# Linear attention followed by a gated feed-forward: PSUM banks named in the order table, two banks per exponential, a finer start, and a last tile in columns

## Chip, cores and metric

One core of one Trainium2 chip. The metric is device microseconds of that core, from the first to the last instruction of one execution. A kernel is run several times and the median of all its runs is quoted. The runs of the kernel before lie within 0.3% of each other. Runs flagged slow (on one core: over 1.5% above the fastest of the same kernel) are left out of the ratios, but not of the medians. "Span" is the length of the one execution that was profiled; here it is some 2 us less than that same run's time.

Before: 393.23 us (392.9 to 394.07, 4 runs).

## The reference, cut to what matters

```python
q, k, v: (8, 8, 576, 64)      w_phi: (64, 128)      # batch, heads, sequence, head_dim
w_gate, w_val: (512, 1536)    w_out: (1536, 512)

def phi(x):
    proj = x @ w_phi
    proj = proj - max(abs(proj), axis=-1)            # kept per row
    return concatenate([exp(proj), exp(-proj)])      # 256 features
                                # (as written, the maximum is subtracted before the sign is turned)
kv  = einsum('bhsf,bhsd->bhfd', phi(k), v);  z = sum(phi(k), over s)
num = einsum('bhsf,bhfd->bhsd', phi(q), kv)
attn = num / (phi(q) . z + 1e-6)                     # (8, 8, 576, 64)

x   = attn.transpose(0, 2, 1, 3).reshape(4608, 512)
out = (relu(x @ w_gate) * (x @ w_val)) @ w_out       # (4608, 512)
```

With `m` the row's largest absolute value, the two halves of phi are `exp(p)·exp(-m)` and `exp(-p)·exp(m)`. So the kernels take the exponentials of the plain projection, and multiply the row factors `exp(-m)` and `exp(m)` into V, which is much smaller. These factors are the tile `ek`.

## The kernel before, in parts

Each batch has 576 positions: 512 are worked in four chunks of 128, and the other 64 (the "tail") of two batches make one mixed chunk. All instructions are issued in an order that was searched beforehand and is written down as a table; PSUM comes from one pool of eight banks.

```python
ORDER = """0 40 41 1 44 45 4 52 53 48 56 57 42 49 ... 735 736 737 738"""   # pieces, in order of issue
LOADS = """km0 q0 wv0 wg0 k1 wv1 wg1 v1 wv2 wg2 q1 wo qm0 k2 km1 vm1 v2 q2 ..."""
...
def order(self):                       # Plan: simulates engines; fills waits of PE with zero matmuls
    ...
        n = int((start - now - 0.25) / (0.43 if now < 8.0 else 0.22))
        if n > 0: ... yield lambda n=n: self.keep_busy(n)
...
def rows_group(T4):                    # K or Q times w_phi: one bank for each parity of heads
    banks = [psum_a(), psum_a()]
    for j in range(4):
        for par in range(2):
            rows = slice(D * par, D * (par + 1))
            nc.tensor.matmul(banks[par][:, F*j : F*(j+1)], lhsT=T4[rows, j, :], rhs=w2[rows, par, :])
    return banks

def k_group(st):
    banks = rows_group(st["T"])
    kp = st["kp"] = st["pool"].tile([P, 2, 4, 2, F], BF16, name="kp")
    for par in range(2):
        row_max(st["m"][:, par::2], banks[par])                     # DVE tensor_reduce, |.|, max
        for s, sign in ((0, 1.0), (1, -1.0)):
            nc.scalar.activation(kp[:, s, :, par, :], banks[par]..., AF.Exp, scale=sign)
    ek = st["ek"] = sb_s.tile([P, 8, 2], FP32, name="ek")
    for s, sign in ((0, -1.0), (1, 1.0)):
        nc.scalar.activation(ek[:, :, s], st["m"], AF.Exp, scale=sign)   # exp(-m), exp(m)

def scale_v(engs, dst, src, ek):       # on POOL: V times the row factors, for both signs
    ...  eng.tensor_tensor(dst[:, :, s, 0:D], src, ek[:, :, s:s+1]..., op=ALU.mult)
...
def q_finish(x, dst, by_dma): ...      # x for the feed-forward, turned by PE or by DMA
def out_step(t, part): ...             # the output projection; one copy on ACT, two stores on SP
...
load_kqv(0, "kn", k, nc.sync, ...)     # first loads; later loads are pieces of ORDER
...
```

From batch 2 on, K and Q are turned by a DMA transpose, issued by SP (`knT<-kn`), and not by PE.

Of the kernel before, what the change touches and what calls it, by code (L numbers as in the profile page):

```python
# [8 lines left out]
FP32 = mybir.dt.float32  # L9
BF16 = mybir.dt.bfloat16  # L10
# [6 lines left out]
FIRST = ((0, 2, 0, 6), (2, 4, 0, 6), (0, 4, 6, 12))  # L17


class Plan:  # L20







    LAG = dict(PE=0.33, ACT=0.2, DVE=0.14, POOL=0.15, SP=0.1, NONE=0.0, DMA=0.0)
    BUSY_TILL = 45.0

    def __init__(self, slots):
        self.slots = {tag: [0.0] * n for tag, n in slots.items()}
        self.free = dict.fromkeys(self.LAG, 0.0)
        self.done = {}
        self.mode = "PE"
        self.uses = {}
        self.pieces = []

    def add(self, rank, kind, fn, ops, needs=(), gives=None, take=(), drop=(), after=(), at=None):


        self.pieces.append((rank, len(self.pieces), fn, ops, needs, gives, take, drop, after, at))

    def times(self, piece):

        _, _, _, ops, needs, _, take, _, after, _ = piece
        if any(n not in self.done for n in needs) or any(n not in self.done for n in after):
            return None
        ready = max([0.0] + [self.done[n] for n in needs])
        for tag in set(take):  # L50
            held = self.slots[tag][: take.count(tag)]
            if len(held) < take.count(tag):
                return None
            ready = max([ready] + held)
        free = dict(self.free)
        ends, start = [], None
        for i, op in enumerate(ops):
            eng, us = op[:2]
            if eng in ("PE", "PE64"):
                us += 0.1 * (eng != self.mode)  # L60
                eng = "PE"
            src = op[2] if len(op) > 2 else i - 1
            t = max(free[eng], ready if src is None or not i else ends[src])
            if len(op) > 4:
                t = max(t, self.done[op[4]])
            if eng == "NONE":
                t = ready if src is None or not i else ends[src]
            if start is None:
                start = t
            free[eng] = t + us  # L70
            ends.append(t + us + (op[3] if len(op) > 3 else self.LAG[eng]))
        return start, ready, ends, free

    def emit(self, piece, got):
        _, _, fn, ops, _, gives, take, drop, _, at = piece
        _, _, ends, self.free = got
        if ops[0][0] in ("PE", "PE64"):
            self.mode = ops[0][0]
        for tag in take:
            self.slots[tag].pop(0)  # L80
        for tag, op, *shared in drop:
            if shared:
                n, key = shared
                ends_ = self.uses.setdefault((tag, key), [])
                ends_.append(ends[op])
                if len(ends_) < n:
                    continue
                self.slots[tag].append(max(ends_))
            else:
                self.slots[tag].append(ends[op])  # L90
        if gives is not None:
            self.done[gives] = ends[-1 if at is None else at]
        return fn

    def order(self):


        assert sorted(map(int, ORDER.split())) == list(range(len(self.pieces)))
        for i in map(int, ORDER.split()):
            piece = self.pieces[i]  # L100
            got = self.times(piece)
            assert got is not None
            now, start = self.free["PE"], got[0]
            if piece[3][0][0] in ("PE", "PE64") and start < self.BUSY_TILL and self.slots["pa"][0] <= now:
                n = int((start - now - 0.25) / (0.43 if now < 8.0 else 0.22))
                if n > 0:
                    self.slots["pa"].append(self.slots["pa"].pop(0))
                    got = self.times(piece)
                    yield lambda n=n: self.keep_busy(n)
            yield self.emit(piece, got)  # L110


ORDER = """0 40 41 1 44 45 4 52 53 48 56 57 42 49 6 46 7 54 58 50 60 14 2 61 71 3 55 43 82 86 62 59 51 5 47 10
83 87 63 64 65 67 90 84 68 69 72 73 9 94 66 88 85 70 13 8 133 74 75 403 404 76 405 78 79 406 407
408 409 410 11 411 80 412 95 89 413 77 109 81 91 98 414 415 416 417 131 418 419 99 420 421 92 422
96 423 93 100 424 425 426 427 97 428 429 127 12 134 128 101 17 142 102 103 430 105 120 431 432 121
433 434 435 106 146 436 437 438 107 110 439 111 440 104 441 442 108 112 135 15 443 116 113 114 444
16 117 445 18 446 132 172 118 447 138 448 122 115 129 449 450 19 119 130 143 144 139 123 451 452
453 454 21 455 456 457 147 150 458 140 182 459 124 136 460 461 161 145 151 148 462 125 463 174 20
141 23 152 464 137 149 212 175 465 153 154 183 22 176 466 467 155 178 186 179 468 469 157 470 471  # L120
184 472 473 162 185 180 158 159 474 173 177 156 163 160 187 475 223 476 164 165 188 213 477 168 478
225 169 214 479 166 238 170 167 171 189 181 480 215 481 190 216 219 25 191 482 483 192 234 484 235
24 485 217 486 193 194 487 220 26 488 489 195 490 226 491 239 27 126 227 221 240 492 493 236 230
197 494 495 496 497 201 498 499 196 202 500 501 218 231 224 222 502 264 278 198 503 504 237 505 228
203 506 232 507 508 199 509 510 200 233 208 29 209 242 229 210 511 270 204 512 274 513 205 241 243
266 206 514 211 207 515 516 244 271 517 518 28 519 265 245 520 246 521 267 282 279 31 522 249 30
253 523 293 315 304 247 524 32 525 526 527 250 272 528 529 254 530 531 280 532 255 268 275 533 534
281 251 535 260 536 537 248 33 318 538 539 540 276 541 256 261 262 542 252 257 543 544 269 326 317
263 545 546 277 258 283 259 327 547 548 549 550 284 551 552 273 553 311 319 34 35 312 554 285 555
37 316 556 286 557 558 36 287 289 559 560 288 290 322 561 294 562 563 356 305 328 564 330 565 295  # L130
323 313 320 566 567 366 568 296 569 570 297 571 572 39 300 573 574 298 575 321 576 345 577 291 578
301 579 580 324 581 302 582 306 331 292 329 299 303 583 358 584 585 307 334 586 362 332 587 588 335
367 589 38 590 333 308 396 591 592 325 397 336 593 594 309 595 337 596 597 310 357 341 363 359 338
598 599 364 600 360 601 602 603 339 370 604 605 606 607 314 371 608 609 610 372 368 611 346 612 342
613 343 347 614 615 340 616 617 618 348 344 352 353 361 354 369 619 620 621 349 350 385 622 374 623
355 351 375 624 625 373 626 627 376 628 629 365 630 381 382 383 631 377 632 633 634 635 386 636 637
638 387 639 640 641 642 392 643 378 393 379 644 645 646 647 648 649 650 651 652 380 653 654 394 388
384 389 390 655 395 656 657 391 658 398 659 660 661 399 400 662 663 664 665 666 667 668 669 670 671
672 673 674 675 676 677 678 679 680 681 682 683 684 685 686 687 688 689 690 401 691 402 692 693 694
695 696 697 698 699 700 701 702 703 704 705 706 707 708 709 710 711 712 713 714 715 716 717 718 719  # L140
720 721 722 723 724 725 726 727 728 729 730 731 732 733 734 735 736 737 738"""

LOADS = """km0 q0 wv0 wg0 k1 wv1 wg1 v1 wv2 wg2 q1 wo qm0 k2 km1 vm1 v2 q2 k3 v3 q3 qm1
k4 km2 vm2 v4 q4 k5 v5 q5 qm2 k6 km3 vm3 v6 q6 k7 v7 q7 qm3"""
# [3 lines left out]
def kernel(  # L148
# [24 lines left out]
    C = 4  # L173
# [15 lines left out]
    sb_k = ctx.enter_context(tc.tile_pool(name="sb_k", bufs=5))  # L189
    sb_kv = ctx.enter_context(tc.tile_pool(name="sb_kv", bufs=16))  # L190
    sb_s = ctx.enter_context(tc.tile_pool(name="sb_s", bufs=6))
    sb_x = ctx.enter_context(tc.tile_pool(name="sb_x", bufs=2))
    sb_h = ctx.enter_context(tc.tile_pool(name="sb_h", bufs=1))
    sb_g = ctx.enter_context(tc.tile_pool(name="sb_g", bufs=4))
    ps_a = ctx.enter_context(tc.tile_pool(name="ps_a", bufs=8, space=bass.MemoryType.PSUM))

    ctx.enter_context(tc.manual_schedule())

    def psum_a(dtype=FP32):
        n = 512 if dtype == FP32 else 1024  # L200
        return ps_a.tile([P, n], dtype, name="pa", tag="pa")
# [760 lines left out]
```

## Time and profile before

| reading | before |
|---|---|
| time, span | 393.23 us, 390.7 us |
| PE busy | 377.9 us, 97% |
| DVE, ACT, POOL busy | 251.6, 244.9, 156.1 us |
| first feed-forward matmul | 35.53 us |
| last matmul's start to the end | 5.20 us |

The page of the kernel before. Its first part gives each engine's busy time, share of the span and instruction count; in part 2 each digit is one fortieth of the span, in tenths of full clock; in part 5 a group of instructions has its count, its busy time and the mean of one in ns, then the engine's idle time ahead of the group.

```profile
span 390.7 us, 8804 instructions
...
PE 377.9 (97%) x3415; PEld 201.3 (52%) x3415; DVE 251.6 (64%) x570; ACT 244.9 (63%) x563; POOL 156.1 (40%) x202
...
PEclk9899999999999999999999999999999999999999
...
L321 ACT ACTIVATE kp<-pa 128x512 bf16<-128x512 f32 x144 | 74.6, 615 | 21.0 <-DVE mk L279 20.6
...
L279 DVE TENSOR_REDUCE mk<-pa 128x4 f32<-128x512 f32 x72 | 45.5, 682 | 7.0 <-PE pa L309 7.0
```

PE is the bound. ACT's 144 exponentials and DVE's 72 maxima of one bank each are long in sum, but ACT and DVE have idle time left. The small exponentials that make `ek`, two per group of K, are in the view of lines:

```profile
L329 ACT ACTIVATE ek<-mk 128x8 f32<-128x8 f32 x72 | 12.3, 244 | 0.0
```

The same execution by stretches: width of the stretch, busy time of PE, PEld, DVE, ACT and POOL with their instruction counts, clock, DMA share and GB/s.

```profile
0.00:26.00 26.00, 21.36 (x235) 12.19 (x236) 15.71 (x34) 17.62 (x45) 18.84 (x32) 0.93 1.05 204
26.00:50.00 24.00, 21.68 (x305) 17.00 (x303) 21.65 (x58) 18.58 (x51) 18.87 (x24) 1.00 1.28 187
...
140.00:320.00 180.00, 179.41 (x1641) 93.13 (x1640) 121.66 (x275) 116.88 (x264) 69.72 (x87) 1.00 0.57 101
```

In the middle PE is idle for 0.6 of 180 us. What is left to gain lies at the start, where "busy" also counts matmuls of zeros that only keep the clock up. For that I counted from the start of each matmul to the start of the next: what goes beyond its columns ÷ 2.4 GHz and some 6 ns is lost, and zero matmuls count apart (in this trace matmuls of 512 columns follow each other every 0.216 us). Before, 22.5 us of the first 50 are lost or zeros, 10.4 us after that, and 352 us of the whole is useful. This is my own count from the trace, not a line of a view; with 2.5 or 8 ns in place of 6 the differences between kernels shift by less than 1 us.

The timeline around the first feed-forward matmul, then the end of the kernel before: start, length, engine, line, operation, and in brackets the idle time ahead of it and what ended that.

```profile
34.73 0.75 DVE L460 COPY xT<-pa 128x512 bf16<-128x512 bf16 x2
...
35.53 0.60 PE L482 MATMUL pf<-xT,wv_sb 128*128 128x256 bf16 x4 [0.27 <-DVE xT L460]
...
384.18 1.67 PE L501 MATMUL pf<-wo_sb,h 128*128 128x512 bf16 x7
384.48 3.18 SPq L518 DMA_DIRECT2D out_dram<-out_sb  x3
...
385.94 0.58 ACT L511 COPY out_sb<-pf 128x512 f32<-128x512 f32 x1 [2.00 <-PE pf L501]
```

### The profile page before, as it was taken

The numbers are of one execution on the slowest core, as the hardware profiler recorded it, in microseconds if no ns is written. First come the engines' busy times: TensorE is split into PE (matmuls) and PEld (weight loads), VectorE is DVE, ScalarE is ACT, GpSimd is POOL, SyncE is SP. The second block draws the span as 40 slices with busy tenths as digits, with TensorE's granted clock in tenths as the row PEclk, the third lists the DMA queues.
The fourth block names the chain that finished last, engine by engine and source line by source line (L and its number), as shares of the span: only waits on it lengthen the run. The fifth ranks groups of instructions, "written<-read, shape, count | busy, mean of one in ns | idle before, by whom it ended". The sixth has DMA issues, their size and how long they took to land.

```text
span 390.7 us, 8804 instructions
## 1 busy us (share of the span) xinstructions
PE 377.9 (97%) x3415; PEld 201.3 (52%) x3415; DVE 251.6 (64%) x570; ACT 244.9 (63%) x563; POOL 156.1 (40%) x202
## 2 busy tenths in 40 slices
PE   6889999999999999999999999999999999999995
PEld 2466764546565445545544455545554444444442
DVE  3789868778898877676756776777557562422420
ACT  2896775579997895779388748677456233323321
POOL 2999442397842487326423653175210120010000
PEclk9899999999999999999999999999999999999999
DMA  7999998499946992899389834530210121011004
GB/s 232 189 169 186 204 183 76 126 183 232 183 107 145 199 161 24 130 219 164 69 107 308 155 40 88 126 58 16 73 65 0 29 81 55 1 62 61 0 15 94
DMA packets 91803, 45.07 MB, mean 115 GB/s; under 512 B 57842, under 2 KB 87154, under 8 KB 91762
## 3 DMA queue, kind: packets, MB, share of 16 engines
q1 hardware_dynamic: 62994, 30.88, 35.8%
q0 software_dynamic: 28768, 13.63, 29.5%
q8 instruction: 27, 0.44, 0.5%
q14 instruction: 14, 0.11, 0.1%
HBM read 37.81 MB, written 9.44 MB: 121 GB/s over the span
## 4 chain that ended last, share of the span: by engine, by line
PE 83%; DVE 6%; DMA 3%; ACT 3%; issue 2%; POOL 1%; SPq 0%; DVEq 0%; POOLq 0%; ACTq 0%
PE pf L482 46%; PE pf L501 20%; PE pa L364 4%; PE pa L415 4%; PE pa L309 4%; PE pa L383 2%; ACT kp L321 2%; DMA out_dram<-out_sb 2%; DVE mq L279 1%; DVE u L439 1%; DMA wf<-in_w_phi_dram 1%; DVE mk L279 1%; DVE t L431 1%; PE pa L271 1%; PE pa L832 1%
## 5 line engine op out<-in xcount | busy, mean ns | idle before, releaser
L493 DVE SCALAR_TENSOR_TENSOR h<-pf,val_sb 128x512 bf16<-128x512 f32 (+1 forms) x114 | 73.9, 658 | 71.7 <-PE pf L482 52.6
L491 ACT CAST val_sb<-pf 128x512 bf16<-128x512 f32 (+1 forms) x114 | 64.0, 583 | 68.1 <-PE pf L482 63.9
L501 PE MATMUL pf<-wo_sb,h 128*128 128x512 bf16 x432 | 101.0, 379 | 0.0
L482 PE MATMUL pf<-xT,wv_sb 128*128 128x512 bf16 (+1 forms) x408 | 99.6, 366 | 0.9 <-DMA out_dram<-out_sb 0.6
L482 PE MATMUL pf<-xT,wg_sb 128*128 128x512 bf16 (+1 forms) x408 | 99.7, 367 | 0.0
L444 POOL TENSOR_TENSOR xu<-u,r 128x512 bf16<-128x512 f32 x36 | 37.5, 1044 | 152.9 <-DVE r L442 108.6
L321 ACT ACTIVATE kp<-pa 128x512 bf16<-128x512 f32 x144 | 74.6, 615 | 21.0 <-DVE mk L279 20.6
L290 POOL TENSOR_TENSOR vs<-vn,ek 128x512 bf16<-128x512 f32 x64 | 65.8, 1050 | 22.2 <-ACT ek L329 14.3
L392 ACT ACTIVATE qp<-pa 128x512 bf16<-128x512 f32 x128 | 66.2, 615 | 6.9 <-PE pa L383 6.8
L482 PEld LDWEIGHTS <-wv_sb 128*128 128x128 bf16 x456 | 42.7, 98 | 43.9 <-issue 1.0
L482 PEld LDWEIGHTS <-wg_sb 128*128 128x128 bf16 x456 | 41.5, 98 | 41.9
L501 PEld LDWEIGHTS <-h 128*128 128x128 bf16 x432 | 38.9, 98 | 42.1
L279 DVE TENSOR_REDUCE mq<-pa 128x4 f32<-128x512 f32 x72 | 45.9, 682 | 17.0 <-PE pa L309 16.9
L279 DVE TENSOR_REDUCE mk<-pa 128x4 f32<-128x512 f32 x72 | 45.5, 682 | 7.0 <-PE pa L309 7.0
L431 DVE TENSOR_TENSOR t<-pa,cq 128x195 f32<-128x195 f32 (+3 forms) x120 | 39.4, 328 | 13.0 <-PE pa L415 11.5
L511 ACT COPY out_sb<-pf 128x512 f32<-128x512 f32 x36 | 21.5, 602 | 37.5 <-PE pf L501 36.0
L439 DVE TENSOR_TENSOR u<-pa,t 128x195 f32<-128x195 f32 (+3 forms) x120 | 40.6, 338 | 6.4
L415 PEld LDWEIGHTS <-qp 128*128 128x128 bf16 x640 | 29.9, 98 | 15.7 <-issue 0.7
L415 PE MATMUL pa<-kv,qp 128*128 128x65 bf16 x640 | 33.2, 193 | 0.6 <-ACT kp L321 0.6
L364 PEld LDWEIGHTS <-kp 128*128 128x128 bf16 x640 | 22.6, 97 | 5.8 <-issue 1.0
L364 PE MATMUL pa<-vs,kp 128*128 128x65 bf16 x512 | 23.4, 193 | 0.8 <-POOL vs L296 0.4
L364 PE MATMUL pa<-vsm,kp 128*128 128x65 bf16 x128 | 20.6, 193 | 0.4 <-POOL vsm L296 0.4
(62 smaller groups left out, 245.4 us busy)
## 6 DMA issues: line engine op xcount, KB each, us to landing
out_dram<-out_sb SPq DMA_DIRECT2D x32, 256.0 KB, 3.0
vn<-in_v_dram SPq DMA_DIRECT2D x7, 1024.0 KB, 8.6
qn<-in_q_dram POOLq DMA_DIRECT2D x8, 512.0 KB, 7.0
kn<-in_k_dram POOLq DMA_DIRECT2D x7, 512.0 KB, 9.3
wg_sb<-in_moe_w_gate_dram POOLq DMA_DIRECT2D x3, 512.0 KB, 9.8
wv_sb<-in_moe_w_val_dram POOLq DMA_DIRECT2D x3, 512.0 KB, 9.6
wo_sb<-in_moe_w_out_dram POOLq DMA_DIRECT2D x1, 1536.0 KB, 18.3
vm<-in_v_dram SPq DMA_DIRECT2D x8, 128.0 KB, 4.1
```

What stands on the lines that cost most here:

```text
L279: nc.vector.tensor_reduce(m, bank.rearrange("p (c f) -> p c f", f=F), axis=AX.X, op=ALU.max, apply_absolute_value=True,)
L290: eng.tensor_tensor(dst[:, :, s, 0:D], src, ek[:, :, s : s + 1].to_broadcast([P, 8, D]), op=ALU.mult,)
L321: nc.scalar.activation(kp[:, s, :, par, :], banks[par].rearrange("p (a f) -> p a f", f=F), AF.Exp, scale=sign,)
L364: nc.tensor.matmul(kv_ps[:, hh, s, :], lhsT=lhsT, rhs=rhs, start=(n == 0), stop=(n == 19))
L392: nc.scalar.activation(x["qp"][:, s, slot].rearrange("p a b -> p (a b)"), cols[par], AF.Exp, scale=sign,)
L415: nc.tensor.matmul(pn[:, E * (2 * i + s) : E * (2 * i + s + 1)], lhsT=x["qp"][:, s, slot, blk, :], rhs=kvs[b, h // 2][:, h % 2, s, :],)
L431: nc.vector.tensor_tensor(t, ab[:, :, 1], st["c"][rows, col(lo) : col(lo + n - 1) + 1 : col(1) - col(0)][:, :, None].to_broadcast([np_, n, ...
L439: nc.vector.tensor_tensor(x["u"][rows, lo : lo + n], ab[:, :, 0], t, op=ALU.add)
L482: nc.tensor.matmul(ps, lhsT=w[:, dc, P * fi : P * fi + P], rhs=xT[:, dc, lo:hi], start=(dc == 0), stop=(dc == NDC - 1),)
L491: nc.scalar.copy(st["val"], ps)
L493: nc.vector.scalar_tensor_tensor(st["h2"][:, fi, lo:hi], ps, 0.0, st["val"], op0=ALU.max, op1=ALU.mult)
L501: nc.tensor.matmul(st["po"], lhsT=st["h2"][:, fi, P * t : P * t + P], rhs=wo_sb[:, fi, :], start=(fi == 0), stop=(fi == NFC - 1),)
```

## The change

Its intent: a start with less waiting, fewer and wider ACT and DVE instructions, and a shorter tail.

1. The eight PSUM banks become one tile; the order table says which bank each piece takes (`43:76` is piece 43 with banks 7 and 6) and where zero matmuls go (`z5:0`). Two neighbouring banks can then be read by one instruction.
2. K's exponentials and maxima, and Q's maxima, read two banks at once (1,024 columns); the products with Q are divided in groups of 7 + 1 heads, not 3 + 3 + 2. The maximum goes straight into half of `ek`, DVE negates it into the other half, and one exponential makes both factors.
3. The first two batches' K tails are worked one batch at a time; later tails stay in pairs, with another layout.
4. The first batch's Q goes one chunk at a time, and its feed-forward in pieces of 128 columns. The first loads are reordered, V of batch 2 is loaded much earlier, and `wo` in three parts.
5. The last 128 output rows are made as columns 256, 128 and 128 wide, copied by DVE and stored from two queues.

The core of the diff; much is cut.

```diff
-ORDER = """0 40 41 1 44 45 4 52 53 48 56 57 42 49 ...
+ORDER = """z5:0 43:76 47:5 0 44:6 51:4 4 48:2 z2:5 59:5 ...
+... 694 699:7 695 702:0 703:1 704:2 696:0 697 698 700 701"""
-LOADS = """km0 q0 wv0 wg0 k1 wv1 wg1 v1 wv2 wg2 q1 wo qm0 k2 km1 vm1 v2 q2 ...
+LOADS = """q0 wv0 wg0 kt1 k1 wv1 wg1 vt1 v1 wv2 wg2 q1 wo0 wo1 wo2 qm0 k2 kt2 vt2 v2 q2 ...
@@ PSUM
+    pall = ps_a.tile([P, 8, 512], FP32, name="pall")
+    def psum_pair():
+        i = plan.banks.pop(0)
+        return pall[:, i : i + 2]
@@ K
-        for par in range(2):
-            row_max(st["m"][:, par::2], banks[par])
-            ... activation(kp[:, s, :, par, :], banks[par]..., AF.Exp, scale=sign)
-        ek = st["ek"] = sb_s.tile([P, 8, 2], FP32, name="ek")
-        for s, sign in ((0, -1.0), (1, 1.0)):
-            nc.scalar.activation(ek[:, :, s], st["m"], AF.Exp, scale=sign)
+        ek = st["ek"] = sb_s.tile([P, 8, 2], FP32, name="ek", bufs=8)[:, 0 : 2 * n]
+        m = ek[:, :, 1].rearrange("p (j i) -> p i j", i=2)
+        for par in range(1 if wide else 2):
+            mine = slice(0, 2) if wide else slice(par, par + 1)
+            other = slice(0, 2) if wide else slice(1 - par, 2 - par)
+            row_max(m[:, mine], banks[:, mine])
+            for s, sign in ((0, 1.0), (1, -1.0)):
+                nc.scalar.activation(kp[:, s, other], banks[:, other], AF.Exp, scale=sign)
+        nc.vector.tensor_scalar(ek[:, :, 0], ek[:, :, 1], -1.0, None, op0=ALU.mult)
+        nc.scalar.activation(ek, ek, AF.Exp)
@@ the tail's factors, zero for the other half of the heads
-        nc.vector.tensor_scalar(ekm..., st["ek"]..., half[:, bb : bb + 1], None, op0=ALU.mult)
+        nc.vector.tensor_tensor(ekm, st["ek"][...], half[...], op=ALU.mult)
@@ last tile
+        def out_last(t, lo, hi):
+            ...
+            nc.vector.tensor_copy(st["last"][:, lo:hi], ps)
+            store_pair(t, st["last"], lo, hi)        # one store from SP, one from ACT
@@ start
+    for hh in range(2):
+        nc.scalar.dma_start(out=wf[D * hh : D * (hh + 1)], in_=w_phi)
```

## The prediction

> **What bounds it now.** TensorE, nearly everywhere. Start to start in the timeline, 512-column matmuls follow each other every 0.216 us, 65-column ones every 0.03; the Trainium skill ("TensorE: Matmul & The Clock Gate", Part 1) gives N ÷ 2.4 GHz + 2.5 ns, and the trace agrees. Counted so (an estimate), the 3,372 useful matmuls need 352 us of the 390.7 us span. The other 39:
>
> - 22.5 us in the first 50 us: PE idle or fed zero matmuls (43 of them). The first feed-forward matmul starts at 35.5 us;
> - about 10 us from 50 to 320 us, mostly gaps near 0.1 us where PE goes between 64-row and 128-row matmuls, hardly a wait;
> - nothing from 320 us to the last matmul; then 4.8 us: a 0.58 us copy on ACT, two stores issued one after the other, landing.
>
> DVE and ACT are 83 to 90% busy from 80 to 140 us (windows), but PE loses little there, so time saved on them is mostly off the path.
>
> **What the change does.**
> 1. Pairs. Of 144 K exps of 512 columns (0.48 us apart) most become 66 of 1024 (estimate 0.85 us); 72 `ek` exps become 37; numerators go in 7+1 heads instead of 3+3+2. ACT 12 to 18 us and DVE 5 to 10 us less busy. Worth 0 to 1.5 us after 50 us.
> 2. The start. Before, POOL is full from 7.9 to 42 us: scaling V (2.3 us a piece) and DMA issues (0.7 to 0.9 us each); the first `xu` comes at 30.0, after four V pieces and two mixed ones. Now K tails of batch 0 come alone (one piece less ahead), POOL's gate opens with an earlier K piece, w_phi loads on ACT's queue (it landed near 5.7 us and held the first weights), and Q goes one chunk at a time. The first `xu` could start near 26.5, xT be ready near 28.5. But the val weights come behind q1 in the queue, and DMA is nearly full till 25 us; their first third was issued at 24.6 and landed at 32.1, now issued near 22 and landing near 30. First feed-forward matmul at 29 to 31. PE work done by then is about 15 us, so 15 us are lost there, plus 2 to 4 up to 50: 17 to 19 instead of 22.5. Gain 3.5 to 5.5 us.
> 3. PE work: tails by two 130-column matmuls, 1 us less; 128-column first batch and one-parity Q chunks, 1.3 us more. Net zero.
> 4. Last tile in columns: a 128-column copy instead of 512 (0.3 us), its stores from two queues (0.5 us). Gain 0.8 us.
> 5. Named banks: another order, no work saved; plus or minus 1 us.
>
> Sum: 5 to 8 us. **Predicted 386.0 us, 80% range 381.5 to 390.5. Faster by over 2% (under 385.4): 0.42; within 2%: 0.56; slower: 0.02.**
>
> **What would show it.** Right: first feed-forward matmul near 30 us, waiting for the val weights' DMA and not for xT; about 23 zero matmuls; ACT and DVE busy time down; PE losses after 50 us unchanged; tail near 4.0 us. Wrong: first feed-forward matmul before 27 or past 33; PE waiting for ACT or DVE over pairs of banks after 50 us.
>
> **What would make it wrong.** Batch 2's V, now loaded early, competing with the weights (the start gains nothing); wide exps holding two banks so that PE stalls in the middle; weights landing earlier than I think (382 us); the clock falling with fewer zero matmuls.

## The result, and the profile after

After: **397.99 us** (396.74 to 398.92, 4 runs), against 393.23 before. The ratio is 1.0116, 95% interval 1.0093 to 1.0139. (A ratio is the mean time of one kernel's fast runs over that of the other's of the same rounds, so not quite the ratio of the medians.) The change was predicted to take about 7 us off; it put 5 us on, and the time lies above the upper end of the predicted range (390.5 us).

The page of the changed kernel, the lines that answer to those shown of before.

```profile
span 395.8 us, 8922 instructions
...
PE 375.1 (95%) x3547; PEld 210.9 (53%) x3595; DVE 256.4 (65%) x459; ACT 236.4 (60%) x440; POOL 153.0 (39%) x168
...
PEclk9996999999999999999999999999999999999999
...
L277 ACT ACTIVATE kp<-pall 128x1024 bf16<-128x1024 f32 (+1 forms) x78 | 70.3, 957 | 22.4 <-DVE ek L241 22.3
...
L241 DVE TENSOR_REDUCE ek<-pall 128x8 f32<-128x1024 f32 (+1 forms) x39 | 44.3, 1135 | 4.0 <-PE pall L259 2.5
```

ACT is 8.5 us less busy. DVE has 111 instructions fewer, and yet is 4.8 us **more** busy. So some DVE instructions take longer than they should. (There are 48 fewer PE records than weight loads: that many matmul records are missing from this trace, so that PE's idle time in it can't be taken from busy time alone. Matched with the complete trace of neg_ekm, all 48 are single matmuls of 512 columns after 66 us.)

The instructions of the new line with the negation, in the changed kernel: count, then the shortest, the median and the longest in ns, and when the first and last started.

```profile
L278 DVE TENSOR_SCALAR ek<-ek x37: 170/173/3597, 9.0 to 264.7; 128x8 f32<-128x8 f32 x35, 128x4 f32<-128x4 f32 x2
```

An operation on 8 numbers in each partition takes 173 ns at the median and 3,597 at the worst. The timeline of the changed kernel shows what it waits for. The record counts this wait as busy time.

```profile
142.61 1.96 POOL L245 TENSOR_TENSOR vs<-vn,ek 128x1024 bf16<-128x1024 f32 x1
...
142.73 1.87 DVE L278 TENSOR_SCALAR ek<-ek 128x8 f32<-128x8 f32 x1
...
146.62 1.92 POOL L245 TENSOR_TENSOR vs<-vn,ek 128x1024 bf16<-128x1024 f32 x1
...
146.96 3.60 DVE L278 TENSOR_SCALAR ek<-ek 128x8 f32<-128x8 f32 x1
...
148.62 1.90 POOL L245 TENSOR_TENSOR vs<-vn,ek 128x1024 bf16<-128x1024 f32 x1
...
150.47 0.62 DVE L383 TENSOR_TENSOR t<-pall,cq 128x455 f32<-128x455 f32 x1
150.65 0.21 ACT L279 ACTIVATE ek<-ek 128x16 f32<-128x16 f32 x1 [1.75 <-DVE ek L278]
...
151.14 1.02 PE L429 MATMUL pall<-xT,wv_sb 128*128 128x512 bf16 x4 [2.72 <-DVE t L383]
```

The first negation starts at 142.73, while POOL scales V, and ends at 144.60, within 0.03 us of POOL's end (142.61 + 1.96 = 144.57). The second waits through two of POOL's products. Behind it in DVE's queue stands a product `t` that frees a PSUM bank, and PE waits 2.72 us for that bank. Thirteen of the 37 negations are longer than 200 ns, and what they take beyond 173 adds up to 10.8 us of DVE. Each of the thirteen ran beside a POOL instruction (eleven a product, two the issuing of a DMA) and ended within 0.04 us of its end; of the other 24 only one lies inside a POOL instruction, a DMA issue.

The Trainium skill has the rule. The page "SBUF — State Buffer", section "Who interferes with whom", says that VectorE and GpSimd share one pair of SBUF ports as an exclusive lock: a one-source `tensor_scalar` from SBUF can take it, the loser blocks fully for the whole instruction, and "Issue order, not op shape, decides who blocks." It also says that `tensor_reduce` never takes it on trn2. The page "VectorE: DVE Perf Modes", section "Mode 2×_2P", names what makes a one-source operation take both ports: source and destination in SBUF, and an even outermost dimension (or an odd one, equal in both). The negation (8 fp32 from SBUF to SBUF) is such a case. The trace agrees: 13 of 37 are lengthened, each beside POOL (it shows the wait, not the mode that the negation ran in). The experiments below test it.

The other places answer to those shown of before. The timeline of the changed kernel around the first feed-forward matmul (PE only), then its end:

```profile
31.46 0.61 PE L401 MATMUL pall<-ident,xu 128*128 128x128 bf16 x4 [1.89 <-POOL xu L391]
...
34.22 1.49 PE L429 MATMUL pall<-xT,wv_sb 128*128 128x128 bf16 x12
...
390.31 1.24 PE L455 MATMUL pall<-wo_sb,h 128*128 128x512 bf16 x5
390.48 2.19 SPq L475 DMA_DIRECT2D out_dram<-out_sb  x2
...
391.59 0.59 ACT L465 COPY out_sb<-pall 128x512 f32<-128x512 f32 x1 [1.14 <-PE pall L455]
392.21 0.50 ACTq L475 DMA_DIRECT2D out_dram<-out_sb  x1
```

The first feed-forward matmul starts at 34.22, not at 29 to 31; PE waits for `xu`, although the first `val` weights landed at 29.74. PE's clock dips in the fourth slice: the trace has it at half from 30.32 to 37.15 us, so the transposes at 31.46 and the first 128-column matmuls of the feed-forward are slower. And the last copy is still one of 512 columns on ACT: the order table puts the column pieces (702 to 704) ahead of the last parts of other tiles.

My count by place; "the mended kernel" is the last one of the experiments. Records are missing in the changed kernel's trace after 50 us, so its starred figure is what is left when the useful work of the mended kernel (the same program in other orders) and the losses of the first 50 us are taken off.

| us | before | after | mended |
|---|---|---|---|
| PE useful | 351.9 | (353.4) | 353.4 |
| first 50 us: lost and zeros | 22.5 | 21.8 | 17.4 |
| after 50 us: lost | 10.4 | about 15.0* | 9.0 |
| last matmul's start to the end | 5.20 | 4.64 | 4.15 |
| span | 390.7 | 395.8 | 384.9 |

### The profile page after: what moved, and what is told of

Read it like the earlier page. It is cut to its first block, busy times and chain, and to the rows that moved or that the text cites. A ratio compares the mean times of both kernels' runs of the same rounds, so it can differ in the third digit from the quotient of the medians.

```text
span 395.8 us, 8922 instructions
## 1 busy us (share of the span) xinstructions
PE 375.1 (95%) x3547; PEld 210.9 (53%) x3595; DVE 256.4 (65%) x459; ACT 236.4 (60%) x440; POOL 153.0 (39%) x168
## 4 chain that ended last, share of the span: by engine, by line
PE 82%; DVE 9%; issue 3%; ACT 3%; DMA 1%; SPq 0%; POOL 0%; DVEq 0%
PE pall L429 43%; PE pall L455 21%; PE pall L374 4%; PE pall L259 4%; PE pall L304 3%; PE pall L338 3%; DVE ek L241 2%; DVE t L383 2%; DVE u L386 2%; DVE h L442 2%; DMA vn<-in_k_dram 1%; PE pall L234 1%; ACT qp L349 1%; PE pall L920 1%; PE pall L312 1%
## 5 line engine op out<-in xcount | busy, mean ns | idle before, releaser
L442 DVE SCALAR_TENSOR_TENSOR h<-pall,val_sb 128x512 bf16<-128x512 f32 x108 | 72.8, 686 | 53.3 <-PE pall L429 48.6
L438 ACT CAST val_sb<-pall 128x512 bf16<-128x512 f32 x108 | 62.9, 596 | 69.8 <-PE pall L429 57.5
L429 PE MATMUL pall<-xT,wv_sb 128*128 128x512 bf16 (+1 forms) x514 | 96.2, 322 | 4.6 <-DVE t L383 2.7
L455 PE MATMUL pall<-wo_sb,h 128*128 128x512 bf16 x402 | 98.1, 379 | 1.1 <-issue 0.3
L429 PE MATMUL pall<-xT,wg_sb 128*128 128x512 bf16 (+1 forms) x514 | 94.7, 321 | 1.9 <-DVE h L442 0.8
L277 ACT ACTIVATE kp<-pall 128x1024 bf16<-128x1024 f32 (+1 forms) x78 | 70.3, 957 | 22.4 <-DVE ek L241 22.3
L245 POOL TENSOR_TENSOR vs<-vn,ek 128x1024 bf16<-128x1024 f32 x32 | 61.1, 1909 | 38.4 <-ACT ek L279 19.8
L241 DVE TENSOR_REDUCE mq<-pall 128x8 f32<-128x1024 f32 x36 | 43.9, 1220 | 23.8 <-PE pall L259 18.7
L241 DVE TENSOR_REDUCE ek<-pall 128x8 f32<-128x1024 f32 (+1 forms) x39 | 44.3, 1135 | 4.0 <-PE pall L259 2.5
L351 ACT ACTIVATE qp<-pall 128x512 bf16<-128x512 f32 x60 | 36.9, 616 | 9.1 <-PE pall L338 9.1
L352 ACT ACTIVATE qp<-pall 128x512 bf16<-128x512 f32 x60 | 37.2, 621 | 0.0
## 6 DMA issues: line engine op xcount, KB each, us to landing
wg_sb<-in_moe_w_gate_dram POOLq DMA_DIRECT2D x3, 512.0 KB, 10.4
```

The costliest lines, as they stand in the source:

```text
L241: nc.vector.tensor_reduce(m, banks, axis=AX.X, op=ALU.max, apply_absolute_value=True)
L245: nc.gpsimd.tensor_tensor(dst[:, :, :, 0:D], src[:, :, None, :].to_broadcast([P, *dst.shape[1:3], D]), ek[:, :, :, None].to_broadcast([P, ...
L277: nc.scalar.activation(kp[:, s, other], banks[:, other], AF.Exp, scale=sign)
L352: nc.scalar.activation(y["qp"][:, s, b], cols[:, 1], AF.Exp, scale=sign)
L429: nc.tensor.matmul(ps[:, n * i : n * (i + 1)], lhsT=w[:, dc, P * fi : P * fi + P], rhs=xT[:, dc, lo:hi], start=(dc == 0), stop=(dc == NDC ...
L438: nc.scalar.copy(st["val", step], ps)
```

## The experiments

Theory: the negation on DVE, which waits for the lock that POOL holds, costs the time. Rivals: the pairs of banks (they hold PSUM longer and make PE wait); the early loads; and the clock. Every ratio is to the kernel before in the same rounds.

### neg_reduce: the same negation by an operation that doesn't take the lock

```diff
-        nc.vector.tensor_scalar(ek[:, :, 0], ek[:, :, 1], -1.0, None, op0=ALU.mult)
+        nc.vector.tensor_reduce(ek[:, :, 0], ek[:, :, 1:2], axis=AX.X, op=ALU.max, negate=True)
```

> The changed kernel with one edit: the negation of the maxima on DVE (a one-source tensor_scalar from SBUF to SBUF, 37 times) becomes a tensor_reduce over an axis of one element with negate, the same numbers at the same place in every engine's order. Lock theory (the tensor_scalar waits while POOL works, 10.8 us in all by the trace of the changed kernel, of which 5 to 8 us reach PE): every negation takes under 0.3 us, the time falls to 390 to 393 us, ratio to before 0.992 to 1.000. Rival (pairs of PSUM banks and the order of the start cost the time, the long negations only fill time that DVE had to spare): the time stays at 396 to 399 us, ratio 1.008 to 1.015.

Measured: 393.26 us over all six runs; the five fast ones lie from 390.02 to 394.57 with a median of 392.17, ratio 0.9979 (0.994 to 1.0018). The first run, 977 us, is slow and left out (the record doesn't say why it took so long); the profile is of that run, so that of it only this is used: the longest of its 37 negations took 164 ns. One instruction, replaced by another of the same result, took 1.4% off (1.0116 to 0.9979). That is the whole loss against the kernel before, but not yet the predicted gain, and its runs spread: two near 390, two near 394, one between.

### neg_act: no negation; two small exponentials on ACT, as before

```diff
-        m = ek[:, :, 1].rearrange("p (j i) -> p i j", i=2)
+        mk = sb_s.tile([P, 8], FP32, name="mk", bufs=8)[:, 0 : 2 * n]
+        m = mk.rearrange("p (j i) -> p i j", i=2)
-        nc.vector.tensor_scalar(ek[:, :, 0], ek[:, :, 1], -1.0, None, op0=ALU.mult)
-        nc.scalar.activation(ek, ek, AF.Exp)
+        for s, sign in ((0, -1.0), (1, 1.0)):
+            nc.scalar.activation(ek[:, :, s], mk, AF.Exp, scale=sign)
```

> The changed kernel with the negation taken out altogether: the maxima go to a tile of their own and ACT takes two exps of them, scale -1 and +1, as the kernel before does (37 more ACT instructions of about 0.2 us). Lock theory: as neg_reduce within 1.5 us, 390 to 394 us. Rival (the extra DVE instruction itself, or pairs of banks): this differs from neg_reduce, or both stay at 396 to 399 us.

Measured: 396.33 us over all six runs (392.99 to 400.61, two of them slow), ratio 1.0111 (1.0069 to 1.0152). The four fast runs average 395.1, which is 1.005 of before; the ratio is higher than they give. A miss either way: the lock is gone here too, and yet little is gained. The runs scatter even more than those of neg_reduce, and only the quickest, the profiled one, is where the theory had it (390 to 394). Something else that changes from run to run must be on the path; it is found further down.

### before_neg: the kernel before, with the negation alone

```diff
+        ek = st["ek"] = sb_s.tile([P, 8, 2], FP32, name="ek", bufs=8)
-            row_max(st["m"][:, par::2], banks[par])
+            row_max(ek[:, par::2, 1], banks[par])
-        for s, sign in ((0, -1.0), (1, 1.0)):
-            nc.scalar.activation(ek[:, :, s], st["m"], AF.Exp, scale=sign)
+        nc.vector.tensor_scalar(ek[:, :, 0], ek[:, :, 1], -1.0, None, op0=ALU.mult)
+        nc.scalar.activation(ek, ek, AF.Exp)
```

> The kernel before with nothing of the change but the negation on DVE and one exp in place of two. Lock theory: some negations last 0.5 to 4 us, each while POOL works, and the kernel gets slower by 1 to 6 us, 394 to 399 us. Rival: within 1 us of before, or faster, since ACT has 36 exps less.

Measured: 398.96 us (398.36 to 399.41), ratio 1.0149 (1.0133 to 1.0165). The negation's instructions in this kernel:

```profile
L327 DVE TENSOR_SCALAR ek<-ek x36: 172/173/1054, 9.0 to 268.5; 128x8 f32<-128x8 f32 x36
```

One part of the change, put into the kernel before, costs 1.5% (5.7 us by the medians). POOL's products are shorter there (512 columns, 1.05 us), and so is the longest negation, 1,054 ns. The kernel has ACT do one exponential less in each of 36 groups, and is slower all the same. So the cause shows from the other side too: taken out of the changed kernel it gives 1.4%, put into the kernel before it takes 1.5%. In this kernel the wait isn't parted from the mere addition of 36 DVE instructions (12 are longer than 200 ns, each beside POOL, and take 6.6 us beyond 173 ns); neg_reduce and clean_lock do that, as they keep the instruction and change only its kind.

### neg_ekm: neg_reduce, and the other DVE operation with two SBUF inputs moved to POOL

```diff
         ekm = sb_s.tile([P, NU, 2, 2], FP32, name="ekm", bufs=2)
-        nc.vector.tensor_tensor(
+        nc.gpsimd.tensor_tensor(
```

> neg_reduce, and the product of the K scales with the half mask (a tensor_tensor with two SBUF inputs on DVE, 8 times, once 1.5 us long in the changed kernel's trace, PE waiting 1 us soon after) moved to POOL. Lock theory: 0.3 to 1.5 us less than neg_reduce. Rival: no less, or more, since POOL has 8 instructions more.

Measured: 392.17 us (389.35 to 394.0), ratio 0.9976 (0.9946 to 1.0006), the same as neg_reduce within the intervals. The negation in its trace:

```profile
L278 DVE TENSOR_REDUCE ek<-ek x37: 158/161/164, 8.7 to 258.8; 128x8 f32<-128x8 f32 x35, 128x4 f32<-128x4 f32 x2
```

The timeline at the place shown of the changed kernel has the reduction run to its end inside a product of POOL, and `t` follow at once:

```profile
143.05 1.91 POOL L245 TENSOR_TENSOR vs<-vn,ek 128x1024 bf16<-128x1024 f32 x1 [1.73 <-ACT ek L279]
...
144.02 0.16 DVE L278 TENSOR_REDUCE ek<-ek 128x8 f32<-128x8 f32 x1
144.10 0.63 DVE L383 TENSOR_TENSOR t<-pall,cq 128x455 f32<-128x455 f32 x1
```

DVE is 244.5 us busy, 11.9 less than in the changed kernel. The moved product had waited once for 1,516 ns in the changed kernel; moving it isn't shown to be worth anything by itself. It stays in all kernels below.

### warm, table, gate, table_warm_z: the start

After neg_ekm I suspected the clock, ACT's table load, and loads that compete at the start.

```diff
 warm:   -65:2 10 92:3 69:70 70:1 66:0 ...
         +65:2 10 z4:3 92:3 69:70 70:1 z6:6 66:0 ...           # zero matmuls in two waits near 27 to 31 us
 table:  +    early = singles.tile([P, 1], FP32)
         +    nc.scalar.activation(early, zeros[:, 0:1], AF.Exp)  # ACT's table load at once
 gate:   -    nc.gpsimd.tensor_copy(gate, inputs["kn", 0][:, 2, 0, 0:1])
         +    nc.gpsimd.tensor_copy(gate, inputs["kn", 0][:, H - 1, 0, 0:1])  # loads later, as before
 table_warm_z: table and warm, and z5:0 -> z2:0 ahead of a piece of K
```

> neg_ekm with ten more zero matmuls where PE stood idle from 26.8 to 30.5 us (four before the third K transposes of batch 1, six before the first transposes of xu). In the changed kernel and in neg_ekm the granted clock is one half from about 30 to 37 us, just when feed-forward starts. Clock theory (idle PE there brings the half clock): the half clock is gone from 30 to 37 us, the first 16 feed-forward matmuls take 0.95 us instead of 1.9, and the time falls by 1.5 to 3 us against neg_ekm (ratio to before 0.990 to 0.994). Rival (the clock falls whatever PE does, or DVE and POOL set the pace there): no change, or 0.5 us more.

> neg_ekm with one exp of one column on ACT right after the w_phi loads, so that the exp table is loaded at 2 us and not at 5.8 us, when the first maxima already wait (it takes 1.28 us and ends at 7.1 in the changed kernel; in the kernel before it is loaded at 0.7 us). Table theory: the first K exps start 0.5 us earlier and the time falls by 0.3 to 1 us. Rival (what comes later, V tails landing and DVE, sets the pace): nothing, within 0.3 us.

> neg_ekm with POOL's first loads (q0, k1) held until the last K piece of batch 0 has landed, as in the kernel before, and not only the second. Theory that early q0 and k1 take DMA time from the V and tail loads that the first batch needs (V tail landed 15.6 us, POOL waits 1.2 us for it in neg_ekm): the V tail lands 1 to 2 us earlier, and the first xu comes up to 1 us earlier; time down 0 to 1 us. Rival (q0 and k1 are needed as early): first xu later, time up 0.5 to 2 us.

> neg_ekm with the early table, the ten zero matmuls, and two instead of five zeros ahead of the first K tail, which run at half clock there and hold the tail's rows back to 13.3 us in the changed kernel, about 0.9 us after its transpose is copied. Theory that these add up: 2 to 4 us less than neg_ekm, 388 to 390.5 us. Rival: no better than warm alone.

| kernel | median us | lowest to highest | ratio (95%) |
|---|---|---|---|
| warm | 396.67 | 392.17 to 397.45 | 1.0048 (1.0003 to 1.0094) |
| table | 393.17 | 390.42 to 396.49 | 0.9956 (0.9908 to 1.0004) |
| gate | 395.94 | 391.63 to 396.91 | 1.0031 (0.9983 to 1.0079) |
| table_warm_z | 397.46 | 391.28 to 398.64 | 1.0013 (0.9943 to 1.0083) |

None of them is told from neg_ekm by its time (the intervals overlap): each has runs near 391 or 392 and runs near 396 or 397. Where the upper runs lie more than 1.5% above the fastest they are left out of the ratio (two of six in table, four of six in table_warm_z), so the ratios of these two kernels rest on few runs; in warm and gate all six count as fast, and spread as much. That spread was the finding. In the trace of `warm`, the half clock near 30 us is gone, and the time is lost somewhere else. Its timeline (PE):

```profile
69.67 0.82 PE L259 MATMUL pall<-w,knT 64*128 64x128 bf16 x12 [1.78 <-DMA knT<-kn]
```

and its chain of waits from 55 to 72 us (start, length, what):

```profile
50.31 19.31 DMA knT<-kn
69.62 0.05 issue
69.67 1.04 PE pall L259 x16
```

In the clock row of its page the eighth slice, which begins near the end of this wait, is low:

```profile
PEclk9999999799999999999999999999999999999999
```

PE waits for batch 2's K to be turned by DMA. That transpose took 19.3 us. It had been issued at 50.31, after two parts of `wo` (49.14 and 49.91), and landed after them. The same transpose, in three other kernels, from the views of DMA issues (count, then us from issue to landing), the changed kernel first:

```profile
wo_sb<-in_moe_w_out_dram POOLq DMA_DIRECT2D x3, 512.0 KB, 10.0
...
knT<-kn SPq DMA_TRANSPOSE x1, 6.2
```

then neg_ekm:

```profile
wo_sb<-in_moe_w_out_dram POOLq DMA_DIRECT2D x3, 512.0 KB, 16.2
...
knT<-kn SPq DMA_TRANSPOSE x1, 13.9
```

In the changed kernel the transpose was issued 0.98 us before the first part of `wo`; in neg_ekm 0.01 us before it; in `warm` 1.17 us after it: 6.2, 13.9 and 19.3 us. When it lands also sorts the profiled runs: landed at 65.28 (neg_ekm), 65.88 (table_warm_z), 65.97 (gate) and 66.22 us (neg_act), the run was one of the quicker group (390.0, 389.5, 389.8 and 391.2 us of span); at 68.67 (table) and 69.62 (warm), one of the slower (394.7 and 395.5). Being behind `wo` does not alone make a run slow: in table_warm_z the transpose was issued 1.44 us after the first part of `wo` and took 17.5 us, but as that was already at 48.41 it still landed at 65.88. That the order of the two differs from run to run, by about a microsecond between SP and POOL, is likely but not shown, with one trace of each kernel.

What the late landing costs can be read by matching matmul for matmul with neg_ekm (my own count): `warm` is 0.6 us ahead at 64 us, 4.1 behind at 69.7 and 5.5 behind from 76 us to the end; table goes from 1.1 ahead to 3.5 and 4.7 behind. So the two slow runs lose their time between 64 and 76 us: most in the wait, and a net 1.3 to 1.4 us at half clock, which follows it in both (67.56 to 74.39 in warm, 66.99 to 73.81 in table) and in none of the four quick ones. In the kernel before K of batch 2 landed at 45.78 and its transpose was issued at 45.80, 6 us after the single load of `wo` (39.79), which landed at 58.14. So the two met there too; when the turn landed isn't in the record, but PE first used it at 69.89, without a wait. Here K landed at 50 to 51, because V of batch 2 was now loaded from about 28 us on, in competition with it.

### late_v, wo_late, late_v_wo: two ways to part them, and both

All on top of `table`.

```diff
 late_v (18 and 19 are the loads of V of batch 2 and of its tail, 130 is the turn of its K):
-... 96:6 100:7 18 381:1 17 16 ... 384:5 19 75:62 ... 77:1 130 15 99:4 ...
+... 96:6 100:7 381:1 17 16 ... 384:5 75:62 ... 77:1 130 18 19 15 99:4 ...
 wo_late (12, 13 and 14 are the three loads of wo):
-... 99:4 12 390:5 13 126 79:7 103:60 118 14 104:1 145 ...
+... 99:4 390:5 126 79:7 103:60 118 104:1 12 13 14 145 ...
 late_v_wo: both
```

> The base is table (no blocked DVE instructions, early exp table). Batch 2's V and V tails are loaded after K of batch 2 is turned, as late as the kernel before does it, and not at 28 to 46 us among the weights. In the runs of the base's family that took 395 to 398 us PE waits 2 to 5 us near 66 to 70 us for the turned K of batch 2, which landed 14 to 19 us after its issue, behind the output weights; where it was issued 1 us ahead of them (the changed kernel) it landed in 6. Theory that V of batch 2 delays K of batch 2 (issued 36, landed 50): K lands 2 to 4 us earlier, its turn is issued ahead of the output weights and lands by 56, the wait is gone and the time settles at 387 to 391 us. Rival (V is not in the way): K lands at 49 to 51 as before, and the runs go on spreading from 390 to 397.

> The base with the three output-weight loads issued 4 to 5 us later on POOL, after the turn of K of batch 2 has been issued; V as in the base. Queue theory (the turn is held behind whatever large loads were issued before it): the turn lands 5 to 8 us after its issue, the wait near 66 us is gone, 388 to 392 us without runs at 396. Rival (turns are slow for another reason): it still takes 14 us or more.

> Both. Queue theory: the turn lands by 54 us, 387 to 390 us with little spread. Rival: spread as in the base, 390 to 397.

| kernel | median us | lowest to highest | ratio (95%) | transpose, issue to landing |
|---|---|---|---|---|
| table | 393.17 | 390.42 to 396.49 | 0.9956 (0.9908 to 1.0004) | 49.83 to 68.67 |
| late_v | 389.39 | 388.3 to 390.59 | 0.9904 (0.9883 to 0.9925) | 45.77 to 50.08 |
| wo_late | 389.79 | 389.27 to 390.17 | 0.9913 (0.99 to 0.9925) | 50.10 to 55.30 |
| late_v_wo | 389.17 | 388.91 to 390.1 | 0.9896 (0.9881 to 0.991) | 46.71 to 50.99 |

Either alone is enough, the two together give no more, and no run lies above 390.6 us. Both leave PE's work as it is; what they have in common is that K's turn is issued well ahead of `wo` (2.75 us in late_v, 6.9 in wo_late) and takes 4 to 5 us. This is also the likely reason for the miss of neg_act: its transpose landed at 66.22 us in the profiled run, which was its quickest, and PE waited 1.78 us for it even there; the others have no trace. That a slow transpose needs the order of issue found here, and not some other traffic of the same moment, isn't separated further.

The view of DMA issues of late_v:

```profile
knT<-kn SPq DMA_TRANSPOSE x1, 4.3
```

### late_v_wo_warm: the clock, now that nothing covers it

```diff
-... 3 2 z5:0 60:6 ...  65:2 10 92:3 69:70 70:1 66:0 ...
+... 3 2 z2:0 60:6 ...  65:2 10 z4:3 92:3 69:70 70:1 z6:6 66:0 ...
```

> Both, and the ten zero matmuls and the shorter cold stretch of table_warm_z. With the turn no longer in the way the clock can be judged: clock theory, no half clock between 13 and 380 us and 1 to 2.5 us less than late_v_wo; rival, the same time within 0.5 us.

Measured: 388.11 us (387.9 to 388.67), ratio 0.9873 (0.986 to 0.9886): 1.1 us under late_v_wo of the same rounds by the medians (the intervals of the ratios, 0.986 to 0.9886 and 0.9881 to 0.991, still overlap a little). There is no half clock between 12.6 and 384.6 us, where late_v_wo has it from 28.7 to 35.6. The page "TensorE: Matmul & The Clock Gate", Part 1, of the Trainium skill gives a window of 3,413 ns after whose idling the array falls to half rate; the interval at half rate in the changed kernel, 6.83 us, is two such windows. But the window needn't be idle in these traces: in the 3.41 us before the clock fell at 30.32, matmuls cover 1.53 us. The edit also takes three zeros away ahead of a piece of K, so the 1.1 us are of both together.

### clean_lock: the negation put back into this kernel

```diff
-        nc.vector.tensor_reduce(ek[:, :, 0], ek[:, :, 1:2], axis=AX.X, op=ALU.max, negate=True)
+        nc.vector.tensor_scalar(ek[:, :, 0], ek[:, :, 1], -1.0, None, op0=ALU.mult)
```

> late_v_wo_warm (388.1 us) with the negation again a one-source tensor_scalar on DVE, as the changed kernel has it. Lock theory: some negations take 0.5 to 3.6 us while POOL works, and the time goes up by 4 to 8 us, to 392 to 396. Rival (most of what neg_reduce gained was luck of the queue): up by less than 2 us.

Measured: 391.88 us (391.01 to 392.58), ratio 0.997 (0.9943 to 0.9997), against 0.9873: the lock costs 1.0%, 3.8 us by the medians, with the transpose out of the way (each against the kernel before on its own chip; I had expected 4 to 8 us, the rival under 2). Thirteen negations are again longer than 200 ns. Its timeline shows the wait pass from engine to engine:

```profile
24.98 1.91 POOL L245 TENSOR_TENSOR vsm<-vt,ekm 128x1024 bf16<-128x1024 f32 x1
...
25.28 1.62 DVE L278 TENSOR_SCALAR ek<-ek 128x8 f32<-128x8 f32 x1
...
26.82 1.21 DVE L241 TENSOR_REDUCE mq<-pall 128x8 f32<-128x1024 f32 x1
...
27.96 0.75 DVE L320 CAST kv<-pall 128x260 bf16<-128x260 f32 x2
28.09 0.40 PE L259 MATMUL pall<-w,tT 64*128 64x128 bf16 x8 [2.05 <-DVE mq L241]
```

The negation is held until POOL's product ends (26.89); DVE's next maximum starts only then, and PE waits 2.05 us for the banks that it frees. The first feed-forward matmul came at 35.24 here, and at 30.85 in the kernel without the lock. Part of that is the clock, which in spite of the zero matmuls is at half from 28.73 to 32.14 us in this trace.

### clean_narrow and clean_narrow2: the pairs of banks taken apart

`clean_narrow` is late_v_wo_warm, and `clean_narrow2` is clean_last (next), with one bank at a time:

```diff
 clean_narrow:   k_group: +        wide = False        # exponentials on the bank whose maximum comes next
 clean_narrow2:  k_group: +        wide = False
 -            other = slice(0, 2) if wide else slice(1 - par, 2 - par)
 +            other = slice(0, 2) if wide else slice(par, par + 1)   # on the bank whose maximum was just taken
```

> late_v_wo_warm with K's exps and maxima one bank at a time, everywhere (144 exps of 512 columns as in the kernel before). ACT about 8 us more busy. The prediction's term (pairs lie off the path): 0 to 1.5 us slower. Rival (pairs are what the change lives on): 2 us or more slower; other rival (pairs hold two banks and make PE wait): faster.

Measured: 403.16 us (403.01 to 403.81), ratio 1.0267 (1.0241 to 1.0292), 15 us slower. This was a bad experiment. The changed kernel's narrow form, meant for its first groups, lets the exponentials read the *other* bank than the maximum, so that DVE's second maximum must wait for ACT. DVE's waits in clean_narrow (us in total, times, longest):

```profile
DVE ek L241 <- ACT kp L278: 25.4, 29, 1.4
```

So the same was run in the bank order of the kernel before.

> The best kernel so far (387.0 us) with K's exponentials and maxima on one bank at a time, and each exponential on the bank whose maximum was just taken, as in the kernel before; the negation stays the reduction. The prediction held that pairing lies off the critical path and is worth 0 to 1.5 us: then 387.0 to 388.5 us here. The rival, that pairing is worth 3 us or more of waiting: 390 us or more. The earlier one-bank run (403 us) is no measure of it, because its exponentials read the other bank, so that the second maximum had to wait for ACT; if this run too shows DVE waiting over 15 us for ACT at that line, the two are not told apart.

Measured: 387.04 us (five runs from 385.96 to 387.64, and one of 394.06 that is over 1.5% above the fastest and so is left out of the ratio as slow), ratio 0.9828 (0.9803 to 0.9853). That is no slower than clean_last (386.99, ratio 0.985), and the intervals overlap. The 25 us of waiting are gone from DVE's list, and ACT is 3.3 us more busy, DVE 2.2 (239.2 against 235.9, 246.2 against 244.0). **K's pairs save busy time, and no time that these runs can tell**; nor do they cost any. Q's maxima stay in pairs in this kernel, so theirs are not tested. Between the two narrow kernels the work is the same, and what differs is which engine waits for which.

### clean_last: the column pieces of the last tile really last

```diff
-... 694 699:7 695 702:0 703:1 704:2 696:0 697 698 700 701"""
+... 694 699:7 695 696:0 697 698 700 701 702:0 703:1 704:2"""
```

> late_v_wo_warm with the three column pieces of the last tile moved to the very end of the order, after the other tiles' last parts. The last copy is then 128 columns wide on DVE (0.29 us) and not 512 on ACT (0.59 us). Theory: from the last matmul's start to the end 0.3 us less, time 0.2 to 0.4 us less. Rival: nothing, the stores' landing hides it.

Measured: 386.99 us (386.04 to 387.9), ratio 0.985 (0.9823 to 0.9876): the best version, faster than both kernels. Against late_v_wo_warm the medians differ by 1.1 us and the ratios by 0.23%, their intervals overlap, and I had expected 0.2 to 0.4. What its trace shows of the end is 0.5 us (from the last matmul's start to the end 4.15 us, and 4.64 before the edit). Its timeline:

```profile
29.28 0.40 PE L401 MATMUL pall<-ident,xu 128*128 128x128 bf16 x4 [0.30 <-POOL xu L391]
...
30.83 1.06 PE L429 MATMUL pall<-xT,wv_sb 128*128 128x128 bf16 x16
...
379.78 1.17 PE L482 MATMUL pall<-wo_sb,h 128*128 128x128 bf16 x18
...
380.99 0.29 DVE L491 COPY out_sb<-pall 128x128 f32<-128x128 f32 x1 [0.26 <-PE pall L482]
```

The last copy now has 128 columns and takes 0.29 us, where it was 512 and 0.59. And the first feed-forward matmul starts at 30.83, as the prediction had it for the change.

## Why the prediction was wrong, point by point

- **The step that failed: "72 `ek` exps become 37 ... ACT 12 to 18 us and DVE 5 to 10 us less busy. Worth 0 to 1.5 us", with "time saved on them is mostly off the path".** Two small exponentials were bought with one negation on DVE, and the prediction doesn't name the negation at all: it was taken as nothing. I didn't ask what else it could wait for. In the runs it waited up to 3,597 ns for POOL, and DVE became 4.8 us more busy where I had it less. The maxima and products behind it in DVE's queue started only as it ended (`t` at 150.47), and those free the PSUM banks that PE waits for. Time *saved* on DVE was off the path, as I had said (clean_narrow2: 0). Time *added* to DVE at a bad moment was on it: +1.5% in the kernel before, -1.4% when taken out of the changed kernel, +1.0% in the mended one. "Off the path" held in one direction only. The Trainium skill's page "SBUF — State Buffer" says which operations take the lock; I had costed by durations alone.
- **"First feed-forward matmul at 29 to 31 ... Gain 3.5 to 5.5 us."** In the changed kernel it starts at 34.22 and the first 50 us lose 21.8 us, where I had 17 to 19: a gain of 0.7. The loads were read rightly (the first third of the `val` weights landed at 29.74, predicted near 30), but the clock and the lock held up the chain to xT. With both mended it starts at 30.83 and 17.4 us are lost. So the estimate of what the start could give was right, and what was missing was what stood in its way: blocked negations (clean_lock: 35.24) and the half clock from 30.32 to 37.15 us.
- **"PE losses after 50 us unchanged."** About 10.4 us before and about 15 after. Matched matmul for matmul with neg_ekm, the same order of work without the lock, the changed kernel falls 0.9 us further behind from 97 to 100 us and 4.1 us from 145 to 154, and no further to the end; the negations at 95.50, 142.73 and 146.96 were blocked just before. So of the nine negations blocked after 50 us, three cost 5.0 us and the others nothing that shows. In the mended kernel the losses are 9.0.
- **"Batch 2's V, now loaded early, competing with the weights"** was on my list of risks, with the wrong victim. It delayed K of batch 2, whose turn by DMA then met the load of `wo`: 14 to 19 us instead of 4 to 7. In the profiled run of the changed kernel itself the turn came just before `wo` and took 6.2 us, so this is not what made that run slow. Once the negation no longer held things up it did count: 4.0 us between the medians of table and late_v_wo (393.17 and 389.17, over all runs), 0.6% or 2.4 us between the ratios of fast runs alone (0.9956 and 0.9896, whose intervals just touch).
- **"The clock falling with fewer zero matmuls"** was named as a risk too and given no size. It fell, and mending it gave 1.1 us by the medians, together with three zeros less. "About 23 zero matmuls" was right (23).
- **"PE work ... Net zero."** By my count 1.5 us more (353.4 against 351.9).
- **"Last tile in columns ... 0.8 us ... tail near 4.0."** 0.56 us and 4.64. The shorter copy brought nothing, because the order table ended with other tiles; only the two store queues did. Put last, the tail is 4.15. I had read the diff of the function but not the last tokens of the table.
- **"Named banks: plus or minus 1 us."** Not tested by itself; every kernel from the changed one on has them.

The sum in the changed kernel, by place: useful work +1.5, start -0.7, after 50 us +4.6, tail -0.6, which is +4.8 of the 5.1 us between the spans. By cause it can't be added up as exactly: the lock is worth 1.0 to 1.4% depending on what else is mended, since a wait that is taken away uncovers another. Mended, the change gives 386.99 us, 1 us from the 386.0 predicted; that doesn't make the prediction right, as it was of the kernel with the lock.

Open: why clean_last gained more than its tail shows (it was run on another chip than late_v_wo_warm, each against the kernel before); whether the exact order of issue or the total traffic makes the transpose slow; what the five runs of neg_act without a trace waited for; and how much the named banks, Q's paired maxima and the wider products do.

## What to carry to other kernels

Before moving a small operation to VectorE, ask what GpSimd is doing then: a 0.17 us operation that can take both SBUF ports lasted, here, to the end of the GpSimd instruction that it met (up to 3.6 us), and delayed what stood behind it; an equivalent that doesn't take them (here a reduction over one element, with the sign turned) never took more than 0.164 us. Look at the longest of a group and not at its mean. When a kernel's runs fall into two groups and no edit seems to matter, look also for two engines that race to issue transfers, and move one of them by several microseconds, as late_v and wo_late did here.

## What the Trainium skill lacked or had wrong

- "SBUF — State Buffer", section "Who interferes with whom": right, and it had the answer. The runs add sizes: a negation of 8 columns goes from 0.17 to 1.87 us behind one POOL product and ends 0.03 us after it. The page's section "Summary: rules for kernel authors" says that the second to issue blocks until the first finishes; here one negation started at 146.96 during a POOL product, and ended at 150.56 after a second product of 1.90 us that POOL had started at 148.62. So the loser can lose twice (3,597 ns). Two of the thirteen blocked negations met the issuing of a DMA by POOL and not a product (253 and 417 ns).
- "VectorE: DVE Perf Modes", section "Mode 2×_2P": the runs fit its conditions; it doesn't speak of the step between elements, and here source and destination have a step of two elements, and the operation was still blocked (13 of 37).
- "DMA: Bandwidth & Descriptors", section "Queues, rings and completion order", has each engine go round the queues packet by packet. It gives no figure for a DMA transpose that competes with loads of another queue: here one of 512 KB took 4.3 us when issued 2.75 us ahead of three loads of 512 KB (late_v), 13.9 when issued at the same moment as the first of them, and 19.3 when issued 1.2 us after it.
- "TensorE: Matmul & The Clock Gate", Part 1: the length of its window agrees (half rate lasted 3.41 or 6.83 us), but its table has the clock fall after an idle window. In the traces here, neg_reduce left out, each of the eleven falls between 12 and 100 us ended a window of 3.41 us in which matmuls cover 26 to 50%, and no window of 52% or more ended in one (my own count, windows laid out from the falls).
